# The eighth pair's attention matmuls in split form: one condition changed in a fused attention and expert kernel

## The chip, the cores and the metric

The kernel runs on one core of a Trainium2 chip. The metric is device time in microseconds, the median of the runs of one program. TensorE (PE in the profile) does the matmuls, and its weight loads are listed apart as PEld; VectorE is DVE, ScalarE is ACT, GpSimd is POOL, and SyncE (SP) issues most of the loads.

## What is computed

An attention layer with a feature map, then two feed-forward layers. Everything is float32.

```python
# 4 batches, 8 heads, 576 tokens, head size 64, 128 features
def phi(x):
    proj = np.einsum('bhsd,df->bhsf', x, w_phi)
    proj = proj - np.max(np.abs(proj), axis=-1, keepdims=True)
    return np.concatenate([np.exp(proj), np.exp(-proj)], axis=-1)
q_p, k_p = (phi(q), phi(k))
kv = np.einsum('bhsf,bhsd->bhfd', k_p, v)
z = np.sum(k_p, axis=2)
num = np.einsum('bhsf,bhfd->bhsd', q_p, kv)
den = np.einsum('bhsf,bhf->bhs', q_p, z)[..., None] + 1e-06
x = num / den                                   # then to 2304 tokens of 512
h = np.maximum(np.maximum(x @ w1, x @ w2), x @ w3)
y = h @ w_out                                   # first expert layer
h = y @ w_in
out = (np.maximum(h, 0.0) + alpha * np.minimum(h, 0.0)) @ w_out2
```

## The kernel before

Two heads of a batch are a pair; there are 16 pairs, four to a batch, and `i_of(pair)` numbers them from 0. The eighth pair is number 7, the last of the second batch. The main loop (L458) goes over the pairs. In each round it loads the next pair (`load_pair`, L145), runs the last pair's queries and this pair's keys together (L465), converts some weight tiles of the first expert layer (`split_w123`, L167; five tiles in the eighth pair's round, by `CONVERT_IN`), and adds three units of that layer (`layer1`, L427), which have 36 matmuls each. The last pair's queries stand in the round after its keys.

`keys` (L272) projects the keys in groups (`exp_keys`, L230: two groups of 256 tokens, then the last 64), takes exponentials, and multiplies them with the values into a PSUM bank, `kvp`. `queries` (L340) does the same projection for the queries, turns the exponentials round with transposes (`pt`, L373), and multiplies them with the result of the keys (`num`, L351; tile `pn`). The numerator and denominator go through POOL's DMAs and become `x`, the input of the expert layer.

There are two forms of the multiplications, chosen by `plain_kv(pair)` (L164):

- In the plain form the operands are ordinary float32. `keys` has 20 matmuls of 128 columns (L298), one for each of five token tiles and four blocks, and copies the bank to `kvf`. `num` multiplies `q` and `kvf` (L270 through `products`).
- In the split form every operand is taken apart into a rounded part and the remainder, both of type float32r: ACT or DVE writes the rounded part (`hi_act` L70, `hi_dve` L73), DVE subtracts (`sub` L76), and three matmuls replace one (`three`, L265). This holds for the values (`vh`, `vl`), the exponentials of the keys (`kh`, `kl`), of the queries (`qh`, `ql`), and the result (`kvh`, `kvl`). `keys` has 30 matmuls of 256 columns (L311). The result lies the other way round, so that four transposes (`kvt`, L330) follow.

A third condition, `plain(pair)`, chooses the form of the projections alone; the first five pairs have the plain one. The tiles `vh` and `vl` also serve as landing tiles of plain pairs' values: an even plain pair's values land in `vl`, an odd one's in `vh`, and a split pair's in a tile `rv` of their own (L148 to L150). The first split pair fills all of `vh` and `vl`, the later ones only the two thirds that change (L276 to L280). The tiles of `kh`, `kl` and `qe` also stage weights (L173, L183).

The order of instructions on each engine is not written by hand. A scheduler sets it when the kernel is built, by its own estimates of time and by the priorities in the code; each engine then works through its list in that order and waits where an input or a buffer is not ready. A change of one pair's operations can therefore move the instructions of others.

```python
        for g, tiles in enumerate(GROUPS):
            pv, mx = project(ops, tiles)
...
            for a in range(4):
                A.activation(ev[:, a, 0], pv[:, a], AF.Exp, bias=mx[:, a : a + 1])
                A.activation(ev[:, a, 1], pv[:, a], AF.Exp, bias=my[:, a : a + 1], scale=-1.0)
```

From the second batch on these exponentials (`ke`) read the projection's PSUM bank (`pj`, two banks) directly; a bank is free when its last reader is done.

Of the kernel before, what the change touches and what calls it, by code (L numbers as in the profile page):

```python
# [21 lines left out]
NPAIR = H // 2  # L22
# [31 lines left out]
def tile_kernel(ctx: ExitStack, tc: tile.TileContext, qT, kT, tails, v, w_phi, w1, w2, w3, w_out, w_in, w_out2, alpha, out):  # L54
# [90 lines left out]
    def load_pair(pair):  # L145

        odd = pair[1] % 2
        tags = ["xh", "rv", "rt", "xl"] if plain(pair) else ["raw", "rv", "rt", "raw"]  # L148
        if plain_kv(pair):
            tags[1] = ("vl", "vh")[odd]  # L150
        shapes = ([P, SM], [P, 5, 3, D], [P, 2 * ST], [P, SM])
        for what, tag, shape, src in sorted(zip("kvtq", tags, shapes, (kT, v, tails, qT)), key=lambda x: ("ktqv" if i_of(pair) else "ktvq").index(x[0])):
            t = at(shape, F32, tag=tag, bufs=2 if tag in ("raw", "xh", "xl") else 1, name=what)
            for part in (slice(0, 2 * P), slice(2 * P, SM)) if what == "k" and i_of(pair) == 0 else (slice(None),):
                nc.sync.dma_start(t[:, part], src[pair][:, part])
            raws[pair, what] = t
# [4 lines left out]
    def i_of(pair):  # L161
        return pair[0] * NPAIR + pair[1]

    def plain_kv(pair):  # L164
        return pair[0] < 2

    def split_w123(f, j):  # L167
        if j == 0:
# [103 lines left out]
    def keys(pair):  # L272

        rv = raws[pair, "v"]
        if not plain_kv(pair):
            if not vs:  # L276
                vs.extend(at([P, 5, 3, D], F32R, tag=tag, bufs=1, name=tag) for tag in ("vh", "vl"))
                part = slice(None)
            else:
                part = slice(None, None, 2)  # L280
            vh, vl = vs
            hi_act(vh[:, :, part], rv[:, :, part])
            sub(V, vl[:, :, part], rv[:, :, part], vh[:, :, part])
        kvp = bank("kv", 1, "kvp")
        first = True
        for tiles, e in exp_keys(pair):
            n = len(tiles) * 512
            if not plain_kv(pair):
                kh = at([P, 1024], F32R, tag="kh", bufs=2, name="kh")
                kl = at([P, 1024], F32R, tag="kl", bufs=2, name="kl")  # L290
                hi_act(kh[:, :n], e[:, :n])
                sub(V, kl[:, :n], e[:, :n], kh[:, :n])
                ops = ((vh, kh), (vl, kh), (vh, kl))
# [652 lines left out]
```

## Time and profile before

| | |
|---|---|
| median of 3 runs | 875.23 us (875.04 to 876.12) |
| the profiled execution | 875.7 us |
| its span, first to last instruction | 873.9 us |
| PE busy | 867.7 us (99%), 6631 matmul records |
| PE weight loads busy | 854.8 us (98%) |
| DVE busy | 683.1 us (78%) |
| ACT busy | 490.4 us (56%) |
| POOL busy | 158.6 us (18%) |
| granted TensorE clock | 1.000 of full speed |

Busy means that at least one instruction of the engine was under way. Matmuls overlap in the engine, so the mean duration of one is longer than the distance from one start to the next. A plain float32 matmul is recorded as two pieces.

### The profile page before, as it was taken

What the parts mean: (1) busy time and instruction counts of PE and PEld (TensorE: products, weight loads), DVE (VectorE), ACT (ScalarE), POOL (GpSimd) and SP (SyncE); (2) the same over time, 40 slices, a digit from 0 to 9 for tenths busy, and PEclk for the clock granted to TensorE, in tenths of its full rate; (3) what the DMA queues carried; (4) which work ended last, traced back from release to release, by engine and by line L of the source; (5) the groups of instructions that cost most, each with busy time, mean ns of one, the idle gap of its engine ahead of it and who ended that gap; (6) DMA issues with size and microseconds to landing.
All of it is one profiled execution on the core that took longest, in us unless ns stands there. A gap on an engine that the chain in (4) does not pass through costs nothing.

```text
span 873.9 us, 17484 instructions
## 1 busy us (share of the span) xinstructions
PE 867.7 (99%) x6631; PEld 854.8 (98%) x6631; DVE 683.1 (78%) x1290; ACT 490.4 (56%) x1017; POOL 158.6 (18%) x278
## 2 busy tenths in 40 slices
PE   9999999999999999999999999999999999999998
PEld 8898999999999999999999999999999999999998
DVE  4579888976888878888999755746478999987781
ACT  4666757677777762334455354646477763544440
POOL 0355222202222235521100101111111000000000
PEclk9999999999999999999999999999999999999999
DMA  6445544223323137996578853746248746533321
GB/s 235 134 165 161 170 125 154 64 63 95 92 74 103 37 115 258 323 320 199 178 247 270 258 174 133 241 168 203 109 138 275 261 153 189 171 123 122 121 74 49
DMA packets 70437, 143.00 MB, mean 164 GB/s; under 512 B 9152, under 2 KB 36176, under 8 KB 70352
## 3 DMA queue, kind: packets, MB, share of 16 engines
q1 hardware_dynamic: 53664, 92.95, 34.3%
q0 software_dynamic: 14816, 45.26, 15.1%
q10 hardware_dynamic: 1872, 3.67, 1.2%
q8 instruction: 52, 0.85, 0.4%
q14 instruction: 33, 0.27, 0.1%
HBM read 93.07 MB, written 46.34 MB: 160 GB/s over the span
## 4 chain that ended last, share of the span: by engine, by line
PE 94%; DVE 3%; DMA 1%; ACT 0%; issue 0%; POOL 0%; DVEq 0%; POOLq 0%; ACTq 0%
PE p L270 26%; PE acc L865 21%; PE sums L777 12%; PE p L679 9%; PE pc L777 6%; PE pj L270 5%; PE pn L270 5%; PE kvp L311 3%; PE pb L777 3%; PE kvp L298 3%; PE pt L373 2%; DVE mx L217 1%; DMA dc<-nd 1%; PE kvt L330 0%; PE warm L135 0%
## 5 line engine op out<-in xcount | busy, mean ns | idle before, releaser
L270 PE MATMUL p<-x,w123t 128*128 128x288 f32 x1728 | 250.4, 298 | 0.0
L270 PEld LDWEIGHTS p<-x,w123t 128*128 128x128 f32 x1728 | 234.8, 188 | 1.4 <-DVE ho L444 0.3
L777 PE MATMUL sums<-x,wi 128*128 128x288 f32 x768 | 107.6, 295 | 0.0
L865 PE MATMUL acc<-wq,o 128*128 128x256 f32 x864 | 105.5, 283 | 0.0
L865 PEld LDWEIGHTS acc<-wq,o 128*128 128x128 f32 x864 | 104.2, 189 | 0.0
L777 PEld LDWEIGHTS sums<-x,wi 128*128 128x128 f32 x768 | 103.9, 188 | 0.0
L865 PE MATMUL acc<-wq,x 128*128 128x256 f32 x648 | 78.1, 280 | 0.0
L865 PEld LDWEIGHTS acc<-wq,x 128*128 128x128 f32 x648 | 77.0, 188 | 0.0
L679 PE MATMUL p<-x,wo 128*128 128x288 f32 x576 | 76.6, 295 | 0.0
L679 PEld LDWEIGHTS p<-x,wo 128*128 128x128 f32 x576 | 76.5, 188 | 0.0
L796 DVE SCALAR_TENSOR_TENSOR g<-neg,al,g 128x576 f32<-128x576 f32 x64 | 50.3, 812 | 23.6 <-ACT neg L795 23.6
L217 DVE TENSOR_REDUCE mx<-pj 128x4 f32<-128x512 f32 (+1 forms) x80 | 49.8, 629 | 15.6 <-PE pj L270 15.3
L785 ACT ACTIVATE s<-sums 128x576 f32<-128x576 f32 x48 | 31.1, 647 | 42.0 <-PE sums L777 41.9
L797 POOL DMA_DIRECT2D g_d<-g x32 | 22.9, 715 | 166.8 <-DVE g L796 144.7
L446 POOL DMA_DIRECT2D h_d<-ho x48 | 27.1, 564 | 123.5 <-DVE ho L444 103.5
L83 ACT ACTIVATE wt<-st 128x512 f32<-128x512 f32 x38 | 25.2, 674 | 36.0 <-DMA st<-in_w_out 18.9
L250 ACT ACTIVATE ke<-pj,mx 128x128 f32<-128x128 f32 x96 | 36.6, 382 | 13.8 <-DVE mx L217 13.6
L795 ACT ACTIVATE neg<-g 128x576 f32<-128x576 f32 x64 | 40.2, 676 | 6.2 <-DVE g L827 5.9
L298 PEld LDWEIGHTS kvp<-v,ke 128*128 128x128 f32 x320 | 40.3, 191 | 2.4 <-ACT ke L251 0.5
L298 PE MATMUL kvp<-v,ke 128*128 128x128 f32 x320 | 42.3, 277 | 0.1
L441 ACT ACTIVATE s<-p 128x288 f32<-128x288 f32 x48 | 19.7, 413 | 40.3 <-PE p L270 36.4
L70 ACT ACTIVATE o<-wt 128x512 fp32r<-128x512 f32 x45 | 27.4, 627 | 25.0 <-PE acc L865 15.9
(161 smaller groups left out, 1819.6 us busy)
## 6 DMA issues: line engine op xcount, KB each, us to landing
g_d<-g POOLq DMA_DIRECT2D x32, 576.0 KB, 4.0
a<-g_d SPq DMA_DIRECT2D x36, 512.0 KB, 4.6
st<-in_w_out SPq DMA_DIRECT2D x22, 512.0 KB, 5.2
wst<-in_w SPq DMA_DIRECT2D x18, 512.0 KB, 4.2
st<-in_w_in SPq DMA_DIRECT2D x16, 512.0 KB, 4.3
yr<-y_d SPq DMA_DIRECT2D x28, 288.0 KB, 3.6
v<-in_v SPq DMA_DIRECT2D x16, 480.0 KB, 4.7
q_d<-wt POOLq DMA_DIRECT2D x28, 256.0 KB, 5.9
```

Of the source, the lines that this page charges most:

```text
L70: A.activation(dst, src, AF.Copy)
L217: V.tensor_reduce(mx, pv, axis=AX.X, op=ALU.max, apply_absolute_value=True, negate=True)
L250: A.activation(ev[:, a, 0], pv[:, a], AF.Exp, bias=mx[:, a : a + 1])
L270: nc.tensor.matmul(dst, x, y, start=i == 0, stop=i == len(ops) - 1, **kw)
L298: nc.tensor.matmul(kvp[:, j * P : (j + 1) * P], e[:, c], rv[:, t, j // 2 : j // 2 + 2].rearrange("p a d -> p (a d)"), start=first, stop=t ...
L446: nc.gpsimd.dma_start(h_d[f, :, o : o + CH], ho)
L679: nc.tensor.matmul(p2[m // 2][1][:, m % 2], x, y, start=k + n == 0, stop=k == NF1 - 1 and n == 2)
L777: nc.tensor.matmul(dst[:, j], a, b, start=start and n == 0, stop=n == len(ops) - 1, skip_group_check=True)
L785: A.activation(s, src, AF.Copy)
L795: A.activation(neg, gv[:, j], AF.Relu, scale=-1.0)
L796: V.scalar_tensor_tensor(gv[:, j], neg, al[:, f + j : f + j + 1], gv[:, j], op0=ALU.mult, op1=ALU.add)
L865: nc.tensor.matmul(acc[i], x, y, start=half == 0 and f == 0 and n == 0 and place[i][1] == 0, stop=half == 1 and f == 3 and n == 2, skip_gr ...
```

## The change

`plain_kv` said yes for the first two batches, pairs 0 to 7. It now says yes for pairs 0 to 6. The eighth pair's values, keys, queries and result are multiplied in split form.

```diff
     def plain_kv(pair):
-        return pair[0] < 2
+        return i_of(pair) < 2 * NPAIR - 1
```

The scheduler moves instructions around this pair. The first place is PE near the sixth pair's last query matmuls (`pn`) and the seventh pair's first key-value matmuls (`kvp`); `p_809`, `p_822` and `p_835` are the three banks of the expert layer's first unit, `pj<-wph,xhk` is the second group of the seventh pair's key projections. Before:

```order
L270 MATMUL pn<-q,kvf 128x320 [waits Activation_49]
L270 MATMUL pn<-q,kvf 128x320
L298 MATMUL kvp<-v,ke 128x128 [waits DMAHW5_49,Activation_49]
L270 MATMUL p_809<-x,w123t 128x288 [waits Activation_49]
L270 MATMUL p_822<-x,w123t 128x288
L270 MATMUL p_835<-x,w123t 128x288
L298 MATMUL kvp<-v,ke 128x128 [waits Activation_49] x4
L270 MATMUL p_809<-x,w123t 128x288 [waits DVE_49]
L270 MATMUL p_809<-x,w123t 128x288
L270 MATMUL p_822<-x,w123t 128x288 x2
L270 MATMUL p_835<-x,w123t 128x288 x2
L298 MATMUL kvp<-v,ke 128x128 [waits Activation_49] x3
```

Of the change:

```order
L270 MATMUL p_809<-x,w123t 128x288 [waits Activation_49]
L270 MATMUL p_822<-x,w123t 128x288
L270 MATMUL p_835<-x,w123t 128x288
L270 MATMUL pj<-wph,xhk 128x256 [waits DVE_49,PE_49]
L270 MATMUL pj<-wpl,xhk 128x256
L270 MATMUL pj<-wph,xlk 128x256
L270 MATMUL pj<-wph,xhk 128x256
L270 MATMUL pj<-wpl,xhk 128x256
L270 MATMUL pj<-wph,xlk 128x256
L373 MATMUL pt<-ident,pp 128x128 [waits Activation_49]
L373 MATMUL pt<-ident,pp 128x128 x3
L298 MATMUL kvp<-v,ke 128x128 [waits Activation_49] x3
```

The six projections, which stood behind the last row of the first list, now stand directly behind the first three layer matmuls, and their first waits for DVE.

The second place is ACT at the same time; `kvf<-kvp` is the copy of the sixth pair's result, `ke<-pj` are the seventh pair's exponentials of the first group. Before:

```order
L250 ACTIVATE ke<-pj,mx 128x128 [waits DVE_49,Activation_49]
L323 ACTIVATE kvf<-kvp 128x512 [waits PE_49]
L83 ACTIVATE wt<-wst 128x512 [waits DMAHW3_49,Activation_49]
L70 ACTIVATE x<-xr 128x288 [waits DMASW6_49,DMASW5_49,DVE_49]
L381 ACTIVATE q<-pt 128x2x256 [waits PE_49]
L382 ACTIVATE q<-pt 128x2x256
L251 ACTIVATE ke<-pj,my 128x128 [waits DVE_49]
```

Of the change:

```order
L250 ACTIVATE ke<-pj,mx 128x128 [waits DVE_49,Activation_49]
L323 ACTIVATE kvf<-kvp 128x512 [waits PE_49]
L70 ACTIVATE vh<-v 128x960 [waits DMAHW7_49,DMAHW4_49]
L83 ACTIVATE wt<-wst 128x512 [waits DMAHW3_49,Activation_49]
L70 ACTIVATE x<-xr 128x288 [waits DMASW6_49,DMASW5_49,DVE_49]
L381 ACTIVATE q<-pt 128x2x256 [waits PE_49]
L382 ACTIVATE q<-pt 128x2x256
```

The rounding of the eighth pair's values is new there, and everything behind it stands one place later.

The third place is DVE at the same time; `pp` is the sum that is the last reader of a projection's bank, `x<-xr` the remainder of the expert layer's input. Before:

```order
L407 TENSOR_TENSOR xr<-nd,xr 128x288
L85 TENSOR_SCALAR wt<-wt 128x512
L76 TENSOR_TENSOR xlq<-q,xhq 128x512
L76 TENSOR_TENSOR x<-xr,x 128x288
L221 TENSOR_TENSOR pp<-pj,mx 128x512
```

Of the change:

```order
L407 TENSOR_TENSOR xr<-nd,xr 128x288
L76 TENSOR_TENSOR xlq<-q,xhq 128x512
L221 TENSOR_TENSOR pp<-pj,mx 128x512
L85 TENSOR_SCALAR wt<-wt 128x512
L76 TENSOR_TENSOR x<-xr,x 128x288
```

The sum moved ahead of a weight conversion (L85) and of the remainder of x.

## Rows read from the trace of the kernel before

**Rows 1.** The page's busy time, share of the span and instructions of each engine.

```profile
PE 867.7 (99%) x6631; PEld 854.8 (98%) x6631; DVE 683.1 (78%) x1290; ACT 490.4 (56%) x1017; POOL 158.6 (18%) x278
```

**Rows 2.** Stretches: us, busy of PE, PEld, DVE, ACT, POOL, clock, DMA share, GB/s.

```profile
60.00:100.00 40.00, 38.44 (x266) 34.82 (x265) 36.15 (x83) 30.04 (x87) 16.40 (x27) 1.00 0.51 157
100.00:160.00 60.00, 60.00 (x441) 57.67 (x440) 51.13 (x120) 38.53 (x95) 16.52 (x30) 1.00 0.43 127
160.00:200.00 40.00, 40.00 (x318) 40.00 (x317) 32.68 (x62) 28.02 (x72) 6.53 (x11) 1.00 0.28 82
```

**Rows 3.** The chain that ended last, plain pieces: start, us, what (two repeats left out).

```profile
94.35 3.96 PE p L270 x30
...
110.99 0.22 PE kvp L298 x2
...
113.09 1.56 PE kvp L298 x14
...
124.03 1.34 PE kvp L298 x12
...
132.92 0.89 PE kvp L298 x8
...
144.08 0.86 PE pn L270 x4
...
152.29 1.08 PE pn L270 x4
...
435.86 76.45 PE p L679 x576
```

**Rows 4.** The same chain: split pieces of the pairs that follow, and a transposed result.

```profile
166.60 1.41 PE kvp L311 x12
...
181.21 0.44 PE kvt L330 x4
...
193.54 0.71 PE pn L270 x6
...
197.26 0.88 PE pn L270 x6
```

**Rows 5.** Groups by shape, 80 to 200 us: names, shapes, count, busy us, mean ns, idle.

```profile
L76 DVE TENSOR_TENSOR kl<-ke,kh 128x1024 fp32r<-128x1024 f32 x5 | 6.1, 1221 | 1.7 <-ACT kh L70 1.7
L76 DVE TENSOR_TENSOR kl<-ke,kh 128x512 fp32r<-128x512 f32 x2 | 1.4, 688 | 1.6 <-ACT kh L70 1.6
L76 DVE TENSOR_TENSOR vl<-v,vh 128x640 fp32r<-128x640 f32 x2 | 1.6, 825 | 0.6 <-ACT vh L70 0.6
L73 DVE CAST qh<-qe 128x1024 fp32r<-128x1024 f32 x1 | 0.7, 686 | 0.0
L76 DVE TENSOR_TENSOR ql<-qe,qh 128x256 fp32r<-128x256 f32 x1 | 0.4, 419 | 0.0
...
L70 ACT ACTIVATE vh<-v 128x960 fp32r<-128x960 f32 x1 | 1.1, 1074 | 0.0
```

**Rows 6.** PE in order of time: start, us, line, operation, idle before and releaser.

```profile
84.38 0.39 PE L270 MATMUL pj<-wph,xhk 128*128 128x256 f32 x1 [0.83 <-DVE ppt L221]
```

**Rows 7.** PE in order of time at the moved projections.

```profile
88.52 0.64 PE L270 MATMUL p<-x,w123t 128*128 128x288 f32 x3
89.25 1.26 PE L298 MATMUL kvp<-v,ke 128*128 128x128 f32 x8
...
91.73 0.36 PE L270 MATMUL pj<-wph,xhk 128*128 128x256 f32 x1
```

**Rows 8.** ACT in order of time in the same stretch.

```profile
87.51 0.46 ACT L70 ACTIVATE x<-xr 128x288 fp32r<-128x288 f32 x1
...
88.79 0.40 ACT L251 ACTIVATE ke<-pj,my 128x128 f32<-128x128 f32 x1
...
90.29 0.45 ACT L251 ACTIVATE ke<-pj,my 128x128 f32<-128x128 f32 x1
```

**Rows 9.** DVE in order of time: the sum that frees the bank.

```profile
90.00 0.68 DVE L221 TENSOR_TENSOR pp<-pj,mx 128x512 f32<-128x512 f32 x1
```

## The prediction

> **What bounds the kernel now.** I read the page's busy table first: TensorE (PE) is busy 99% of the span and its weight loads 98%, with VectorE (DVE) at 78% [rows 1]. A busy PE is not a full PE, so the second view is the table of stretches around the change. From 100 to 160 us, where the eighth pair is worked on, PE is busy all 60.00 us at granted clock 1.00, that is 2.4 GHz; DVE has 51.13 of 60 and ScalarE (ACT) 38.53 [rows 2]. Third, the chain that ended last: from 94 us on it runs through PE piece after piece, and the eighth pair's own matmuls are pieces of it [rows 3]. So in this stretch a microsecond of PE work taken out is a microsecond of time, as long as nothing new makes PE wait. From 60 to 100 us that is not so: PE is busy 38.44 of 40 us [rows 2], and it waits 0.83 us behind a DVE result at 84.38 us [rows 6]. That is how a wait looks here when DVE has 36.15 of 40 us to do.
>
> The median of the runs is 875.23 us. The rows come from one execution of 875.7 us: its span of 873.9 us and 1.8 us around it. I make the sum as a difference from that execution and take it off the median, which lies 0.5 us lower. A difference of 0.2%, 1.75 us, is about what a measurement of this kernel can tell from no change.
>
> **PE work removed and added.** Plain, the eighth pair has 20 key-value matmuls, recorded as 40 pieces of 128 columns. In the chain they are 14, 12 and 8 records for 1.56, 1.34 and 0.89 us, and three times two records at 0.22 us [rows 3]: 4.45 us. Its queries have 16 records: two pieces of four at 256 columns, 0.86 us each, and two of four at 320 columns, 1.08 us each [rows 3]: 3.88 us. Together 8.33 us.
>
> Split, the rows of the next pairs give the price. Twelve key-value matmuls of 256 columns take 1.41 us [rows 4], so 30 take 3.53. Four transposes of the result, which the plain form does not need, take 0.44. Query matmuls: six take 0.71 us (256 columns) and six 0.88 us (320 columns) [rows 4]; twelve of each make 1.42 and 1.76. Together 7.15 us. **Net: 1.2 us less PE work.** It is small because three products of one pass stand against one product of two recorded passes.
>
> By weight loads the result would be another. Plain needs 40 + 16 = 56 loads, split 30 + 24 + 4 = 58. If each load set the pace at the 1.56/14 = 0.11 us of [rows 3], the change would add 0.2 us of PE work. The rows speak against it: per record, a piece takes 0.11 us at 128 plain columns and 0.27 us at 320 [rows 3], so columns set the pace. The Trainium skill (Perfetto Trace Analysis, Identifying the Most-Contended Engine) tells one to judge TensorE by the busy share of its weight loads and not by that of its matmuls; by that rule the change gains nothing on PE. The trace disagrees for these shapes: 0.11 against 0.27 us a record with the same load.
>
> **Work added on DVE and ACT.** DVE gets two subtractions of the keys at 1.22 us and one at 0.69, one for the result at the same 0.69, two for the queries like the keys' large ones and one at 0.42, one rounding at 0.69, and one of the values at 0.83 (the full one of 960 moves from the ninth pair to the eighth, the ninth gets the short one) [rows 5]: 2.44 + 0.69 + 0.69 + 2.44 + 0.42 + 0.69 + 0.83 = 8.2 us. DVE's idle time from 100 to 160 us is 60 - 51.13 = 8.9 us, and from 160 to 200 us another 7.3 [rows 2]. I cost the 8.2 us at nothing, covered by that idle time and by matmuls of the first expert layer that stand between a result and its reader. The cover can be counted at the first place: between the eighth pair's first key-value matmuls and the first that reads the first new subtraction, the new order has 48 layer matmuls, 6.3 us at the 3.96/30 of [rows 3]. If the cover is gone, PE waits; that is the rival below. ACT has 21 us idle there; of its additions only one matters.
>
> **The moved copy.** The eighth pair's rounding of the values, 1.07 us on ACT [rows 5], is placed directly behind the sixth pair's result copy. Its data is there: the load moves from the 41st to the tenth place in SP's queue, into a tile nobody held, and takes the place of an equal load. Behind it on ACT stand a weight conversion, the copy of x that ends at 87.51 + 0.46 = 87.97 us, and the seventh pair's exponentials from 88.79 us [rows 8]; all move by about 0.9 us, since neighbours overlap a little. PE's three layer matmuls at 88.52 us [rows 7] wait for x and begin near 88.9, done at 89.35.
>
> Next on PE now comes the second group of the seventh pair's key projections, moved ahead of 13 other matmuls. In its row it waits for DVE, for the sum that frees a bank. Two DVE operations fewer stand ahead of that sum: it began at 90.00 us and took 0.68 [rows 9], and now begins about 0.7 earlier and ends near 90.0. PE goes on at about 90.05, where it had gone on at 89.25 [rows 7]: 0.8 us lost. Some 0.2 comes back, since the stretch that follows, from 89.25 to 91.73, held 2.3 us of matmuls in 2.5 us. **I take 0.6 us.** The ends are 0 (the old gap before 89.25 and later ones absorb it) and 2.4 us (the bank were the one that the exponentials free: their last began at 90.29 and would end near 91.65 against 89.25 [rows 7, 8]).
>
> Can PE pass the waiting matmul by? At 84.38 us it did not: 0.83 us idle with ready work behind it [rows 6]. The Trainium skill (TensorE: Matmul & The Clock Gate, Part 3, The mechanism) says that matmuls start and end strictly in program order, and only weight loads are pulled ahead; the trace agrees with that 0.83 us. If they could pass, the term would be 0.
>
> **Sum:** -1.2 + 0 + 0.6 = -0.6 us. The profiled execution would be 875.1, the median **874.6 us**.
>
> **The rivals.**
> - *The gain comes through whole, and more.* No wait at 89 us, and the new order closes the small gaps between pieces, such as the 0.2 us above at several places. Then -1.2 - 0.7 = -1.9: 873.3 us. For it: the whole stretch from 100 us shows no idle PE, so the order is well covered. Against it: little is left there to close. Chance 0.13.
> - *DVE becomes the bound (slower).* The eighth pair's iteration also converts five weight tiles on DVE, and 51.13 + 8.2 = 59.3 of 60 us would be full. If the idle time is waiting that repeats, the 8.2 us push results behind their readers. Price: with DVE at 90%, PE lost 40 - 38.44 = 1.56 us in 40 us [rows 2], so at least 2.3 us in 60, up to twice that when fuller: 876.9 to 879.2. It decides for slower once PE waits more than about 2.4 us in all beyond my sum, and the first place to see it is the eighth pair's key-value matmuls waiting for the first subtraction of the keys. Against it: ACT and PE are in step with DVE, and from 140 to 200 us split pairs run with PE full. Chance 0.16.
> - *The bank is freed by the exponentials.* -1.2 + 2.4 = +1.2: 876.4 us, still no difference. Chance 0.06.
> - *Weight loads set the pace.* +0.2 + 0.6 = +0.8: 876.0 us. Chance 0.04.
> - *The change does not do what it says.* The new order has 140 plain and 270 split key-value matmuls where there were 160 and 240, so it does; no chance.
>
> **How the numbers follow.** The forecast, 874.6, has 0.61; its own range with the bounds of the wait (0 to 2.4 us) is 874.0 to 876.4. It, the bank and the weight loads are within 0.2% of 875.23 (873.5 to 877.0): 0.71 less 0.03 for a median that falls just outside. Faster: 0.13 and 0.01 of that. Slower: 0.16 and 0.02. The range that holds 8 in 10 reaches to the first rival and to the near end of the second: 873.3 to 877.3 us.
>
> **What the profile would show.** Right: 40 + 16 plain records fewer, 30 + 24 + 4 split ones more, PE full from 100 to 340 us, DVE near 59 of 60 us from 100 to 160, and one new wait of PE near 89 us behind the DVE sum, 0.5 to 1 us. Wrong: waits of PE behind DVE between 110 and 180 us (the second rival), a wait near 89 us behind ACT of over 2 us (the third), or the matmuls of the first expert layer's output starting nearly 2 us earlier than 435.86 us [rows 3] (the first).

## The result and the profile after

The changed kernel takes 883.93 us (881.9 to 886.5 in six runs) against 875.45 us for the kernel before beside it: a ratio of 1.0099, 95% interval 1.0088 to 1.0110. It is slower by 8.5 us. The forecast was 874.6 us, with a range that ended at 877.3. The profiled execution took 883.28 us.

The page's busy table of the changed kernel, then its stretches (columns as in [rows 2]):

```profile
PE 869.6 (99%) x6633; PEld 856.7 (97%) x6633; DVE 690.3 (78%) x1299; ACT 493.7 (56%) x1024; POOL 158.4 (18%) x278
```

```profile
60.00:100.00 40.00, 37.97 (x269) 34.59 (x268) 36.38 (x84) 31.73 (x89) 17.04 (x27) 1.00 0.47 145
100.00:160.00 60.00, 56.48 (x408) 54.09 (x407) 49.88 (x114) 32.60 (x81) 14.76 (x27) 0.99 0.45 135
160.00:200.00 40.00, 39.31 (x301) 38.81 (x301) 34.61 (x65) 29.39 (x73) 6.43 (x12) 0.97 0.19 54
```

The whole-span shares of [rows 1] hardly move, and show nothing. The stretches do. From 100 to 160 us PE is busy 56.48 us where it was busy all 60.00, and with 408 records in place of 441. And DVE, to which the change gives more work, is busy *less* than before over the whole stretch: 49.88 us against 51.13 [rows 2]. The 60 us hide two halves. From 100 to 140 us DVE is fuller than before, and from 140 to 160 us, where PE is short of work, it is busy 13.55 of 20 us in place of 17.68 (stretches before, then of the changed kernel):

```profile
100.00:140.00 40.00, 40.00 (x304) 38.76 (x303) 33.45 (x78) 24.82 (x65) 9.45 (x17) 1.00 0.47 136
```

```profile
100.00:140.00 40.00, 40.00 (x291) 38.52 (x290) 36.33 (x83) 24.01 (x62) 13.67 (x25) 1.00 0.45 131
140.00:160.00 20.00, 16.48 (x119) 15.57 (x118) 13.55 (x32) 8.59 (x19) 1.08 (x2) 0.97 0.45 143
```

Behind 200 us the kernel before keeps PE full until its last matmuls, but for 0.03 us. The changed kernel has one more wait, at 389.16 us, where a layer matmul waits for DVE's `ho`, the output of a unit of the expert layer (PE's waits, 200 to 500 us: total, times, longest):

```profile
PE p L270 <- DVE ho L444: 1.1, 1, 1.1
```

The chain that ended last shows where the loss starts:

```profile
143.32 0.47 PE kvp L311 x4
...
149.36 0.60 DVE kvl L76
...
152.32 0.60 DVE wt L91
153.03 0.63 ACT w123t L70
153.68 0.70 DVE w123t L76
...
157.19 1.06 ACT kh L70
...
443.42 76.45 PE p L679 x576
```

Before, the chain ran from 94 us on through PE alone. Now it leaves PE at 148.9 us and runs through DVE and ACT until about 177 us, but for one piece of PE: the last step of the eighth pair's result (`kvl`), then weight conversions one after another, with the ninth pair's casts and operations of the queries between them. A second time it leaves PE from 343.5 to 389.16 us, for transfers and work of POOL, ACT and DVE, up to the wait for `ho`; before, it stays on PE there. The first matmul of L679 starts at 443.42 us in place of 435.86 [rows 3], 7.6 us later; its 76.45 us are the same.

What PE did in order of time (the count behind x says how many matmuls a row joins):

```profile
89.41 0.36 PE L270 MATMUL pj<-wph,xhk 128*128 128x256 f32 x1 [0.56 <-DVE pp L221]
...
123.03 0.28 PE L311 MATMUL kvp<-kh,vl 128*128 128x256 f32 x1
123.14 2.31 PE L270 MATMUL p<-x,w123t 128*128 128x288 f32 x16
...
128.24 1.22 PE L270 MATMUL p<-x,w123t 128*128 128x288 f32 x8
...
130.13 3.57 PE L270 MATMUL p<-x,w123t 128*128 128x288 f32 x24
133.54 0.28 PE L311 MATMUL kvp<-kl,vh 128*128 128x256 f32 x1
...
153.70 0.53 PE L270 MATMUL p<-x,w123t 128*128 128x288 f32 x2 [1.02 <-ACT w123t L70]
154.43 1.58 PE L270 MATMUL p<-x,w123t 128*128 128x288 f32 x10 [0.19 <-DVE w123t L76]
158.30 0.39 PE L311 MATMUL kvp<-kh,vh 128*128 128x256 f32 x1 [2.29 <-ACT kh L70]
```

The wait near 89 us is there, as forecast. Between the eighth pair's second key-value matmul and the first that reads a subtracted key stand 16 + 8 + 24 = 48 layer matmuls, the ones I had counted as cover. No wait of PE is recorded there. The waits come 20 us later, when PE needs a converted weight at 153.70 us and the ninth pair's first keys at 158.30 us.

Now DVE in the changed kernel, the subtractions of the keys and of the weights (`w123t` is the last step of a conversion):

```profile
120.95 0.68 DVE L76 TENSOR_TENSOR w123t<-wt,w123t 128x512 fp32r<-128x512 f32 x1
...
127.89 0.68 DVE L76 TENSOR_TENSOR w123t<-wt,w123t 128x512 fp32r<-128x512 f32 x1
...
129.83 1.22 DVE L76 TENSOR_TENSOR kl<-ke,kh 128x1024 fp32r<-128x1024 f32 x1
...
135.89 1.23 DVE L76 TENSOR_TENSOR kl<-ke,kh 128x1024 fp32r<-128x1024 f32 x1 [0.97 <-ACT kh L70]
...
137.97 0.68 DVE L76 TENSOR_TENSOR w123t<-wt,w123t 128x512 fp32r<-128x512 f32 x1
...
139.60 0.68 DVE L76 TENSOR_TENSOR kl<-ke,kh 128x512 fp32r<-128x512 f32 x1
```

and ACT:

```profile
118.99 1.14 ACT L70 ACTIVATE kh<-ke 128x1024 fp32r<-128x1024 f32 x1
...
144.48 0.58 ACT L327 ACTIVATE kvs<-kvp 128x512 f32<-128x512 f32 x1
...
148.16 0.60 ACT L70 ACTIVATE kvh<-kvt 128x512 fp32r<-128x512 f32 x1 [0.95 <-PE kvt L330]
148.66 0.66 ACT L83 ACTIVATE wt<-wst 128x512 f32<-128x512 f32 x1
```

The first key subtraction starts at 129.83 us, 10.8 us after its cast at 118.99. It comes soon after the end of a weight conversion (the twelfth, last step at 127.89 us), and the third, at 139.60, soon after the end of the next (last step at 137.97). `wt`, the weight in conversion, and `kl` share two buffers (both have the tag "kl"). That the subtractions come late because of this is a reading of the order here; experiment 8 tests it. The key result is late, and the fourteenth weight conversion, next on ACT behind `kvh`, starts at 148.66 us. Before, it started here:

```profile
137.58 0.74 ACT L83 ACTIVATE wt<-wst 128x512 f32<-128x512 f32 x1
```

That is 11 us earlier. Last, the clock behind the wait of 2.29 us (stretches of the changed kernel):

```profile
156.00:158.00 2.00, 0.01 (x1) 0.00 (x0) 1.05 (x2) 0.81 (x1) 0.00 (x0) 1.00 0.05 18
158.00:160.00 2.00, 1.68 (x7) 1.48 (x8) 1.16 (x3) 1.33 (x3) 0.00 (x0) 0.70 0.00 0
160.00:162.00 2.00, 2.00 (x10) 2.00 (x10) 1.68 (x3) 0.16 (x1) 0.00 (x0) 0.50 0.00 0
162.00:164.00 2.00, 2.00 (x16) 2.00 (x15) 0.52 (x1) 2.00 (x5) 0.00 (x0) 0.95 0.00 0
```

PE does almost nothing from 156 to 158 us, and from 158 to 162 us the granted clock is 0.70 and then 0.50, its level of 1.2 GHz. That costs at most 2 x (0.30 + 0.50 + 0.05) = 1.7 us. Of the six runs of this kernel the one with a mean clock of 1.000 took 881.9 us, and the five with 0.998 took 883.3 to 886.5.

The account of the 7.6 us: idle PE in the three stretches is 0.47 + 3.52 + 0.69 = 4.7 us more than in [rows 2], the wait at 389 us adds 1.1, and the lower clock 1.7, together 7.5. With the 1.2 us of work saved there must be 8.8, so some 1.3 us do not show as idle time or clock in these rows. A busy PE is not a full one.

### The profile page after: what moved, and what is told of

It is laid out like the page before. It is cut to its first block, busy times and chain, and to the rows that moved or that the text cites. A ratio compares the mean times of both kernels' runs of the same rounds, so it can differ in the third digit from the quotient of the medians.

```text
span 881.5 us, 17508 instructions
## 1 busy us (share of the span) xinstructions
PE 869.6 (99%) x6633; PEld 856.7 (97%) x6633; DVE 690.3 (78%) x1299; ACT 493.7 (56%) x1024; POOL 158.4 (18%) x278
## 4 chain that ended last, share of the span: by engine, by line
PE 88%; DVE 4%; DMA 3%; issue 2%; ACT 1%; POOL 1%; SPq 0%; POOLq 0%; DVEq 0%; ACTq 0%
PE acc L865 20%; PE p L270 19%; PE sums L777 12%; PE p L679 9%; PE pj L270 6%; PE pc L777 6%; PE pn L270 5%; PE kvp L311 3%; PE pb L777 3%; PE kvp L298 3%; PE pt L373 2%; DMA st<-in_w_out 1%; DMA xr<-r_d 1%; DMA nd<-nd 1%; DMA v<-in_v 1%
## 5 line engine op out<-in xcount | busy, mean ns | idle before, releaser
L679 PE MATMUL p<-x,wo 128*128 128x288 f32 x576 | 76.6, 295 | 0.0
L679 PEld LDWEIGHTS p<-x,wo 128*128 128x128 f32 x576 | 76.5, 188 | 0.0
L251 ACT ACTIVATE ke<-pj,my 128x128 f32<-128x128 f32 x96 | 38.3, 399 | 4.8 <-DVE my L248 4.7
L362 ACT ACTIVATE nd<-pn 128x256 f32<-128x256 f32 (+1 forms) x64 | 27.1, 429 | 22.0 <-PE pn L270 21.2
```

Source lines behind the costliest of these rows:

```text
L679: nc.tensor.matmul(p2[m // 2][1][:, m % 2], x, y, start=k + n == 0, stop=k == NF1 - 1 and n == 2)
```

## The experiments

Every kernel was timed beside the kernel before, which had 875.1 to 875.3 us. "Own buffers" means that a tile leaves the shared tag. Each edit also makes the scheduler write a new order on all engines, so a result belongs to the edit and its order together.

**1. Raw weights out of `kh` and `qe`.**

```diff
-        tag = ("kh", "qe")[len(unfetched) % 2]
+        tag = "wst"
```

> The changed kernel, but the raw weight tiles (wst) have two buffers of their own in place of the kh and qe buffers. Theory A (shared buffers): after the change the eighth pair's kh tiles hold the two buffers into which the last weight tiles are to be loaded, so these loads go out behind that pair's kvp matmuls (141.28, 144.10 and 153.18 us in place of 132.95 and 143.66 for the last two before), the last five conversions start at 148.7 to 169.4 us in place of 137.6 to 160.2, and PE runs out of layer matmuls. Freed, the last load goes out by about 145 us and the time comes back to 874 to 877. Theory B (work): the split form's 8 us of extra work on DVE and 3 us on ACT is what delays the conversions; buffers change nothing and the time stays 882 to 885. Theory C (values): the ninth pair's value load and its vh, vl copies wait for the eighth pair's kvp matmuls and hold up ACT and DVE; time stays 882 to 885.

Measured: 886.76 us, ratio 1.0132 (1.0115 to 1.0149). Theory A falls in this form. The edit leaves two buffers for raw weights where there were four, and PE waits 5.6 us for converted weights (PE's waits of this run, 130 to 200 us: total, times, longest):

```profile
PE p L270 <- ACT w123t L70: 5.6, 3, 3.6
```

**2. The keys alone, and the queries alone.** A second condition, `plain_q`, chooses the form of the queries; the result of the keys is copied once, or taken apart, as the queries need it.

```diff
+    def plain_q(pair):
+        return pair[0] < 2
...
-        parts = ("q",) if plain_kv(pair) else ("qh", "ql")
+        parts = ("q",) if plain_q(pair) else ("qh", "ql")
```

> Half of the change: the eighth pair's keys and values in split form, its queries in plain form (kvt copied once, as 32-bit values). Theory A: the loss stays, as the kh tiles are in the raw weights' buffers: 881 to 885. Theory B: kl, kvl and vl are some 4.7 of the 8 us of extra DVE work, so some 5 of the 8.5 us of loss: 879 to 881. Theory C: as A, 882 to 885.

> The other half: the eighth pair's queries in split form, its keys and values in plain form (kvh and kvl made straight from kvp). Theory A: no kh tile in the eighth pair, so the raw weights are loaded as before; the qe tiles come after the conversions: 874 to 877. Theory B: ql and kvl are some 3.5 of 8 us of DVE work: 878 to 880. Theory C: the values stay plain, so 874 to 876.

Measured: keys alone 880.28 us, ratio 1.0057 (1.0041 to 1.0074); queries alone (the two conditions exchanged) 877.65 us, ratio 1.0028 (1.0017 to 1.0040). The keys carry more, 5.2 us against 2.6. B's ranges miss the second by 0.4 us and hold the first, A's miss both by 0.7 us and C's by 1.7, so this favours B without settling it. With the keys alone the first subtraction starts 10.8 us after its cast, as in the changed kernel.

**3. One conversion moved from the eighth round to the fifth.**

```diff
-CONVERT_IN = (0, 1, 1, 2, 2, 3, 4, 5)
+CONVERT_IN = (0, 1, 1, 2, 3, 3, 4, 4)
```

> The changed kernel with one weight tile more converted in the fifth round and one less in the eighth (0,1,1,2,3,3,4,4 for 0,1,1,2,2,3,4,5). Theory A: four weight tiles in place of five sit behind the eighth pair's kh tiles; conversions start about 5 us apart, so the last is ready some 5 us earlier and about half of the loss goes: 877 to 881. Theory B: the same work on DVE is spread over more rounds: 880 to 884. Theory C: the value tiles are as they were: 882 to 885.

Measured: 883.88 us, ratio 1.0104 (1.0080 to 1.0127): no gain. The fourteenth weight is ready 12 us earlier (its last step at 141.57 in place of 153.68 us), the other four within 3.1 us of where they were. So the number of conversions in that round is not the cause by itself.

**4. Own buffers for converted weights and for half of the raw ones.**

```diff
-        wt = at([P, 512], F32, tag="kl", bufs=2, name="wt")
+        wt = at([P, 512], F32, tag="wt", bufs=2, name="wt")
...
-        tag = ("kh", "qe")[len(unfetched) % 2]
+        tag = ("wst", "qe")[len(unfetched) % 2]
```

> The changed kernel with buffers of their own for the converted weights (wt, no longer in kl's) and for that half of the raw weights (wst) that lay in kh's, so that no key tile of the eighth pair shares a buffer with a weight. The run with two buffers for all raw weights did not tell this, as it also halved the raw weights on their way. Theory A2 (shared buffers): the fourteenth conversion can't start before the kvp matmuls have read kl (about 141 us; it starts at 148.7 against 137.6 before); freed, the last five conversions start again from 138 us on, and the time is 874 to 877. Theory B (work): the eighth pair's own casts and subtractions take their turn on ACT and DVE before the conversions, whoever owns the buffers: 880 to 885. Theory D (chain): the fourteenth conversion stands in ACT's row behind kvh, which waits for the transposes of kvs and they for the layer matmuls ahead of them; with own buffers it comes before kvh and half of the loss goes: 877 to 881.

Measured: 877.29 us, ratio 1.0023 (1.0014 to 1.0033): 883.93 - 877.29 = 6.6 of the 8.5 us are back. The time is 0.3 us above A2's range and inside D's, but not for D's reason: the fourteenth conversion still stands right behind `kvh` on ACT, only all of it is earlier (139.64 us). B is out as the main cause here.

**5. The subtractions on POOL.** In the eighth pair `kl`, `ql` and `vl` are computed by POOL.

```diff
-                sub(V, kl[:, :n], e[:, :n], kh[:, :n])
+                sub(G if i_of(pair) == 2 * NPAIR - 1 else V, kl[:, :n], e[:, :n], kh[:, :n])
```

> The changed kernel with the eighth pair's low parts of keys, values and queries (kl, ql, vl) subtracted on POOL, which is busy for 2 of 40 us there, in place of DVE: about 7.5 of the 8 us of added DVE work leave DVE. On POOL one 128x288 subtraction took 0.815 us in this trace, so one of 1024 takes about 2.9 us by that rate. Theory B (DVE's work): the time comes back to 874 to 878, less what the slower subtraction costs at the kvp matmuls. Theory A2 or D (buffers, chain): the buffers and the order of ACT's row are as they were, and the low parts come 1.7 us later each: 884 to 890.

Measured: 891.66 us, ratio 1.0190 (1.0175 to 1.0205), above A2's own range. It does not test theory B, because POOL does not take the work off DVE. POOL and then DVE of this run in order of time:

```profile
136.32 2.40 POOL L76 TENSOR_TENSOR kl<-ke,kh 128x1024 fp32r<-128x1024 f32 x1
```

```profile
136.53 2.74 DVE L76 TENSOR_TENSOR xlk<-k,xhk 128x512 fp32r<-128x512 f32 x1
```

The DVE subtraction beside it takes 2.74 us; the same one takes 0.68 us alone (138.93 us in the changed kernel). It ends only after POOL's, so the work that POOL takes over still keeps DVE.

**6. Conversions spread more evenly** (`CONVERT_IN = (0, 1, 2, 3, 3, 3, 3, 3)`).

> The changed kernel with the weight conversions spread as 0,1,2,3,3,3,3,3 over the first eight rounds in place of 0,1,1,2,2,3,4,5: fifteen conversions in place of thirteen stand ahead of the eighth pair's keys on ACT, three in place of five behind them. Moving only one, by 0,1,1,2,3,3,4,4, changed nothing, as the last four kept their times. Theory B or D (whatever delays the last ones, they are late behind the eighth pair's keys): with two of five ahead the first waiting PE reads come about 10 us later: 876 to 880. Theory A (loads): the last loads still wait for kh buffers: 882 to 885.

Measured: 881.17 us, ratio 1.0071 (1.0056 to 1.0086), just over the range of B and D and under that of A. PE loses 2.6 us more than before in 60 to 100 us (35.83 us busy in place of 38.44), so it gives back early what it gains late.

**7. The work alone.** To the kernel before, the eighth pair's casts and subtractions are added, into tiles that nothing reads.

```diff
+            if i_of(pair) == 2 * NPAIR - 1:
+                extra(e[:, :n])
             yield
```

> The kernel before, with the eighth pair in plain form, and in addition the split form's casts on ACT and subtractions on DVE of its values, keys and queries, into two tiles of their own that nothing reads (kvs, kvh, kvl and the transposes are not added). Theory B (work): the added 6.5 us on DVE and 5 us on ACT cost what the change cost: 881 to 885. Theory A2 or D: no shared buffer is taken and PE waits for none of it: 875 to 878.

Measured: 880.82 us, ratio 1.0067 (1.0045 to 1.0090). Between the two, 0.2 us under B: work whose results nobody reads costs 5.6 us. The last conversion's last step starts at 178.03 us, where before it is at 171.59, and PE waits 2.2 us for converted weights. The granted clock falls here too (0.72, 0.50 and 0.92 in the three slices of 2 us from 172 us on, at most 1.7 us), and PE waits 1.2 us for `ho` at 389.60 us: together 5.1 of the 5.6 us. The added tiles have one buffer each, where the keys' parts of the split pair have two; ACT waited 0.5 us for that.

**8. The two halves of experiment 4 apart.**

> Half of the run that brought 6.6 of 8.5 us back: only the converted weights (wt) have buffers of their own, the raw weights stay in kh's and qe's. If kl's buffers are what holds the fourteenth conversion (theory A2, wt and kl), 877 to 879. If the raw weights must come in ahead as well (the fifteenth's and sixteenth's loads go out at 127 and 141 us, behind kvp matmuls that read kh), 880 to 884. By the order in which ACT's row is now written, the fourteenth conversion still stands behind kvh, so I expect the second.

> The other half: only the raw weights leave kh's buffers, wt stays in kl's. If kh's buffers are what delays (theory A, loads), 877 to 879. If kl's buffers hold the fourteenth conversion until the kvp matmuls at 141 us (theory A2), 881 to 885: its conversion starts behind kvh, near 148 us. If either buffer alone is enough to hold it, own_wt and this run both stay at 880 to 885.

Measured: `wt` alone 877.15 us, ratio 1.0024 (1.0013 to 1.0035); raw weights alone 888.24 us, ratio 1.0158 (1.0142 to 1.0173). The one line on `wt` is the whole of the gain, 883.93 - 877.15 = 6.8 us. The raw weights alone are 3.2 us above the range of the second theory; in that trace PE waits 1.9 us for a converted weight and 2.8 us for `ho` at 389.89 us, and why stays open. For `wt` I had expected the other outcome, since the fourteenth conversion still stands behind `kvh` on ACT. It does, but `kvh` itself is 4.2 us earlier. DVE and ACT with own `wt`:

```profile
122.20 1.22 DVE L76 TENSOR_TENSOR kl<-ke,kh 128x1024 fp32r<-128x1024 f32 x1
123.33 0.68 DVE L76 TENSOR_TENSOR w123t<-wt,w123t 128x512 fp32r<-128x512 f32 x1
...
128.37 1.23 DVE L76 TENSOR_TENSOR kl<-ke,kh 128x1024 fp32r<-128x1024 f32 x1
...
135.39 0.69 DVE L76 TENSOR_TENSOR kl<-ke,kh 128x512 fp32r<-128x512 f32 x1 [0.17 <-ACT kh L70]
```

```profile
120.25 1.14 ACT L70 ACTIVATE kh<-ke 128x1024 fp32r<-128x1024 f32 x1
...
144.00 0.65 ACT L70 ACTIVATE kvh<-kvt 128x512 fp32r<-128x512 f32 x1
144.48 0.73 ACT L83 ACTIVATE wt<-wst 128x512 f32<-128x512 f32 x1
```

The first key subtraction now starts 2.0 us after its cast, in place of 10.8, and *ahead* of the eleventh conversion (123.33) and the twelfth, both of which it stood behind. PE, which waited at 153.70 and 158.30 us, has no recorded wait between 91 and 174 us here. In all six kernels that keep the two shared buffers and subtract the keys on DVE, the first key subtraction starts 0.9 to 1.9 us after the start of a conversion's last step, which is the last reader of that `wt` buffer. So the sharing did its harm in a direction that none of my theories had: the keys wait for the weights' buffers, and the next weights are late as a consequence.

DVE's load alone does not explain the loss: it is nearly as full with own `wt` (100 to 140 us, columns as above; the changed kernel had 36.33):

```profile
100.00:140.00 40.00, 40.00 (x290) 38.41 (x289) 35.80 (x82) 25.21 (x64) 10.74 (x20) 1.00 0.44 124
```

**9. Both own buffers and the early conversion; own buffers in the kernel before.**

> Own buffers for both, and one conversion moved from the eighth round to the fifth (0,1,1,2,3,3,4,4). With the buffers free, what is left of the loss is the eighth pair's work on DVE (19.5 of 20 us busy in 120 to 140), ahead of conversions that come 2 to 4.6 us later than before the change. Theory B for the rest: one conversion less behind it brings 1 to 3 us, 874 to 876.5, and with PE's 1.2 us of saved work 873.5 at best. If the rest is PE's wait for pp and the like near 90 us (1.9 us more in 60 to 100 than in the changed kernel's gain would leave), nothing: 876.5 to 878.

> The kernel before with the same own buffers for wt and that half of wst. No key tile in split form is written before the ninth pair there, so theory A2 has the buffers free already: 874.5 to 876.5, no difference. If own buffers help by themselves (any weight conversion, any pair), 871 to 874.

Measured: 875.03 us, ratio 1.0000 (0.9990 to 1.0009), and 875.66 us, ratio 1.0007 (0.9998 to 1.0016). The move that brought nothing with shared buffers brings the last 2 us without them. Own buffers by themselves are worth nothing to the kernel before. In that run the last conversion's last step starts at 184.74 us, 13 us later than in the kernel before without them, and PE is busy all of 160 to 200 us. So a late conversion is not a loss by itself; it costs where PE's order asks for the weight sooner.

**10. The work alone with own `wt`; three shared buffers.**

> The kernel before with the added casts and subtractions of the work run (+5.6 us), and with own buffers for the converted weights (wt), so that kl of the ninth pair on doesn't share with them. Theory E (the added work costs only as far as conversions and key tiles wait for each other's buffers): 876.5 to 878.5, what the split pair costs with own buffers. Theory B (work costs by itself, whoever owns the buffers): 879.5 to 882.

> The changed kernel, wt and kl still sharing, with three buffers in place of two. Theory A2 (two buffers for key parts and converted weights are one too few): the third key subtraction no longer stands behind the thirteenth conversion (135 us in place of 139.6 us) and the time is 876.5 to 878.5, as with own buffers. If the sharing itself, not their number, delays (each weight still takes its turn behind a key tile): 880 to 884.

Measured: 882.82 us, ratio 1.0084 (1.0069 to 1.0100), and 881.76 us, ratio 1.0075 (1.0060 to 1.0091). Theory E falls: the added work costs 7.6 us in the order written for it, though nothing of the eighth pair shares a buffer. A third shared buffer brings the third subtraction to 136.25 us as expected, but the first still starts 8.9 us after its cast (127.93 against 119.03), and most of the loss stays. Own buffers help where one more shared buffer does not.

**11. Attempts to beat the kernel before.** Own buffers, the early conversion and the first cast of the values on POOL; own `wt` with the early conversion; own `wt` with the conversion moved to the third round (0, 1, 2, 2, 2, 3, 4, 4) or the fourth (0, 1, 1, 3, 2, 3, 4, 4).

> Own buffers for both, one conversion moved to the fifth round, and the first cast of the eighth pair's values on POOL in place of ACT at 86 us. In that run (875.0) PE waited 1.4 us for pp sums in 60 to 100; with the cast off ACT's row that wait goes: 873 to 874.5, faster than before. If the wait comes from DVE's own row, not from the cast: 875 to 876.

> Own buffers for the converted weights alone (the least edit that brought the loss back to 2 us), with one conversion moved from the eighth round to the fifth. Own buffers for both with that move gave 875.0; the raw weights' buffers made no difference without it (877.15 and 877.3): 874.5 to 876. If the earlier fetch needs the raw weights' own buffers, 877 to 879.

> Own buffers for the converted weights, and the conversion taken from the eighth round goes to the third (0,1,2,2,2,3,4,4), where DVE is busy 13.7 of 20 us (40 to 60), not to the fifth. With it in the fifth PE waited 1.0 us at 81.6 us for a pp sum of DVE, and the time was 875.4. If that wait is what keeps the split form's gain of 1.2 us on PE from showing: 873.5 to 874.8. If another wait takes its place, as in every run so far: 875 to 877.

> The same with the conversion in the fourth round (0,1,1,3,2,3,4,4), nearer to the stretch of 60 to 80 where DVE is busy 18.1 of 20 us. If the wait at 81.6 us goes here too: 873.5 to 874.8; if DVE in 60 to 80 is filled by it and PE waits for a pp sum there, 875 to 876.5.

Measured: 876.14 us, ratio 1.0007 (0.9998 to 1.0016); 875.38 us, ratio 1.0003 (0.9994 to 1.0012); 880.23 us, ratio 1.0064 (1.0050 to 1.0079); 880.60 us, ratio 1.0066 (1.0054 to 1.0078). None beats the kernel before. Every one moves the wait rather than ending it. With the conversion in the fifth round PE waits early (own `wt` and the early conversion, PE in order of time):

```profile
81.67 0.36 PE L270 MATMUL pj<-wph,xhk 128*128 128x256 f32 x1 [1.00 <-DVE pp L221]
```

With it in the third round that wait is gone, and PE waits at 57 us and loses 2 us around 190 (PE in order of time, and stretches); with it in the fourth PE is idle 3.2 us in 60 to 100 and 1.7 in 160 to 200. The rows of the third:

```profile
57.16 1.13 PE L270 MATMUL pj<-wraw,k 128*128 128x256 f32 x4 [1.08 <-ACT ke L251]
```

```profile
40.00:60.00 20.00, 18.75 (x119) 16.34 (x118) 16.60 (x32) 14.95 (x38) 12.44 (x21) 1.00 0.55 180
80.00:100.00 20.00, 19.56 (x135) 17.80 (x135) 16.46 (x45) 17.46 (x52) 5.39 (x10) 1.00 0.44 109
180.00:200.00 20.00, 18.03 (x136) 16.75 (x136) 16.45 (x33) 14.41 (x39) 5.24 (x10) 1.00 0.32 102
```

All kernels with the eighth pair's keys split on DVE in one table: the wait of that pair's first key subtraction, from the start of its cast to its own start, and the start of the last conversion's last step, both from the profiled execution of each.

| kernel | time, us | first key subtraction after its cast, us | last conversion, us |
|---|---|---|---|
| changed | 883.93 | 10.8 | 179.23 |
| own buffers, raw weights only (two) | 886.76 | 33.1 | 183.59 |
| own buffers, half of the raw weights | 888.24 | 24.3 | 181.61 |
| keys only | 880.28 | 10.8 | 178.28 |
| conversion early | 883.88 | 18.3 | 182.28 |
| conversions even | 881.17 | 12.1 | 176.48 |
| three shared buffers | 881.76 | 8.9 | 182.29 |
| own `wt` | 877.15 | 2.0 | 176.05 |
| own `wt` and half of raw | 877.29 | 1.6 | 174.96 |
| the same, conversion early | 875.03 | 4.1 | 169.82 |
| the same, first value cast on POOL | 876.14 | 2.8 | 169.47 |
| own `wt`, conversion early | 875.38 | 1.1 | 171.81 |
| own `wt`, conversion in the third round | 880.23 | 1.7 | 173.15 |
| own `wt`, conversion in the fourth round | 880.60 | 1.2 | 174.55 |

All those that share `wt` with `kl` wait 8.9 us or more and take over 880 us. Those with own `wt` wait 4.1 us at most, and take 875 to 877 us unless a conversion is moved to the third or fourth round; these two take 880 us for some other reason, which no run isolates, as the subtraction hardly waits in them. The size of the wait does not give the time (33.1 us goes with 886.76, 24.3 with 888.24).

## Why the prediction was wrong

**The step that failed** is the one that read: "I cost the 8.2 us at nothing, covered by that idle time and by matmuls of the first expert layer that stand between a result and its reader." Three things were wrong in it.

First, the buffers. The text ahead of the prediction says that the tiles of `kl` also stage weights, and the sum has no term for it. A key part now holds one of two buffers from its subtraction to its last matmul, and a weight holds one for its whole conversion: the thirteenth from 127.42 us (ACT) to 137.97 + 0.68 = 138.65 us (DVE). Key parts stand behind conversions, and the next conversions behind the result of the keys. Own buffers for `wt` alone take 6.8 of 8.5 us away (experiment 8). That is the largest part, shown by an edit of one line; the same buffers change nothing in the kernel before (experiment 9).

Second, the cover. I counted 48 layer matmuls ahead of the first reader as proof that the subtraction had room. They were there, all 48. But they are the sign of the delay, not a reserve: the order puts them there where the subtraction comes late. Between the same two matmuls stand 39 to 153 layer matmuls in the kernels that share `wt` with `kl`, and 7 to 16 in those with own `wt`. That they are missing at 153 to 158 us, because they were used up at 123 to 134, is my reading; no run moves them alone.

Third, the idle time. 8.9 us of idle DVE in 60 [rows 2] is not room for 8.2 us of work: DVE goes through its list in order, and what it is given is taken from what stands behind. Work that nobody reads costs 5.6 us (experiment 7).

**The steps that held.** The new wait near 89 us, forecast behind the DVE sum with 0.5 to 1 us, is there at 89.41 us with 0.56, and PE is idle 0.47 us more in 60 to 100, where the sum had 0.6. PE has two records more, as counted (58 for 56). PE's pieces have the forecast prices: 12 split key-value matmuls take 1.41 us in the changed kernel's chain, as in [rows 4]. DVE's added work is 690.3 - 683.1 = 7.2 us of the 8.2. The saved 1.2 us on PE never showed in a time: no kernel with the split eighth pair was measurably faster than the kernel before.

**The rivals.** "DVE becomes the bound" had the right sign at 0.16, with 876.9 to 879.2 us. Its condition, that DVE's idle time is waiting and not room, is the third point above. As a bound it did not happen: it forecast DVE at 59.3 of 60 us, and DVE was busy 49.88, full only from 100 to 140 us (36.33 of 40), and with own `wt` nearly as full there at a loss of 2 us. It forecast PE waiting at the first subtraction, where PE has no recorded wait. The rival with the right mechanism, two users of two buffers, was not on the list. The gain in whole and the exponentials are out: the wait at 89 us was behind DVE and short. Weight loads forecast 876.0 us, and nothing here points to them; no run tests them. Of the signs named for being right, PE full from 100 to 340 us and DVE near 59 of 60 us failed.

**What stays open.** Why the work alone costs 5.6 us (7.6 with own `wt`), while the split pair with own `wt`, which has the same work and more, costs 2.0: each kernel gets its own order on all engines, and no run here holds the order fixed. And 1.3 us of the loss show in no idle time and no clock of the rows.

## What to carry to other kernels

Before costing added work at nothing, list the buffers its tiles rotate through and who else uses them, and price the time for which each user holds one; a tag with two buffers and two users is a resource like an engine. In an order written by a scheduler, independent work between a producer and its reader is a sign that the producer is expected late, so count what that work was needed for later. And look for the loss where the stretch runs out of ready work, not where the change sits: here 20 to 30 us behind it, and once more at 389 us.

## What the runs showed of the hardware

A two-input subtraction on POOL holds up a two-input one on DVE: 2.74 us in place of 0.68, beside a POOL operation of 2.40 us (experiment 5). Two weight steps with two inputs (L89) took 2.36 and 2.42 us beside POOL's later subtractions, in place of 0.68. Beside two others, DVE operations with one tensor input were held too: L248 on 128x4 took 2.34 us in place of 0.16, and L85 2.03 in place of 0.41. One that reads an operand from PSUM (L442, at 141.26 us, within a POOL subtraction of 1.31 us) took its usual 0.46. The Trainium skill (GPSIMD Engine Reference, 8. Key points) says that POOL shares its SBUF interfaces with VectorE and contends with instructions that have two SBUF inputs or run in a 2-port performance mode. The trace agrees on the two inputs, and shows DVE held for nearly the whole POOL operation; whether the one-input operations ran in such a mode no run here shows.

A shortage of buffers need not show as idle time. DVE sat idle 1.0 us in all before the three key subtractions, though the first started 10.8 us after its cast. The Trainium skill (Perfetto Trace Analysis, Optimization Strategy) says that a gap repeating on the engine that should be full can mean too few buffers for the next tile. By that sign nothing would have been found here: DVE had other work in its list, and the gaps came on PE, later and only in places.
